# Loading a weight in half rows, and the new plan that goes with it, in an attention and gated-MLP kernel

## The chip, the cores and the metric

The kernel runs on one core of a Trainium2 chip. The metric is the device time of one execution in microseconds, the median of several runs. The engines are PE (matrix multiply), ACT, DVE and POOL (elementwise work) and SP, which here only issues DMAs. The chip has two PE clock levels, 1.2 and 2.4 GHz; the profile gives the granted clock as a share of the higher one.

## The reference

Attention over a band, then a gated MLP on its output, for 8 batches of 576 rows, 8 heads of 64, float32 throughout except `w_in` and `w_out`, which arrive as float64:

```python
scores = scale * np.matmul(q, k.transpose(0, 1, 3, 2))
scores = np.where(masks[None], scores, -1e9)       # band of 32; heads 4 to 7: every 4th of 128
attn = softmax(scores)                             # with 1e-9 added to the sum
x = np.matmul(attn, v)                             # (8, 576, 512) after the heads are joined
h = np.maximum(x @ w_in, 0.0)                      # w_in 512 x 1024
u, v = h[..., :512], h[..., 512:]
v_n = (v - mean(v)) / np.sqrt(var(v) + 1e-6)
v_s = np.einsum('ts,bsd->btd', w_spatial, v_n) + b_spatial[None, :, None]
out = (u * v_s) @ w_out                            # w_out 512 x 512
```

## The kernel before

Everything is kept as a high and a low float32r part, and a product is three matmuls (high-high, high-low, low-high). For each batch the program makes scores and softmax in units of three blocks of 64 rows (`unit`: scores L600, mask L631, the maximum's correction L665, the exponential L675, the transposes L615), weights the values (`weighted`, L750), splits the result into `xth`/`xtl` (`evacuated`, L791 on ACT and the subtraction on DVE), multiplies with the v half of `w_in` (`v_tile`, L815), normalises, multiplies with the u half (`gate`, L882) and with the spatial weights (L892), and projects (`project`, L917). Two head pairs make a group G; a batch has two groups of three units each.

The weights need work of their own before they can be used. A chunk c of `w_in` is 128 rows of 1024 float64 words (1 MB), in two transfers of 64 rows, one to partitions 0 to 63 and one to 64 to 127. `weight` turns one half of a chunk (512 columns, u or v) into float32r parts, in eight steps on ACT (L449, L479, L484), DVE (L453, L455) and, by the table `BY_POOL`, POOL or DVE: an 'a' there puts the addition on POOL (L462) and else on DVE (L465), an 's' puts the subtraction that gives the low part on POOL (L382) and else on DVE (L379). A chunk's staging buffer is given back when both its halves have been read, and then takes the spatial weights and `w_out`.

The order of the instructions on each engine is not the scheduler's. A planner (`Timeline`) holds a cost for each step, picks the next step by its earliest start plus a weight on its rank, and the program keeps the order that comes out; `SHIFTS` adds a number to the rank of each strand, `LOADS` lists the first transfers in the order in which SP is to issue them. Each engine then runs its list in order, and an instruction that waits holds up all behind it. While nothing else is ready in the first 20 us of the plan, `warm` fills PE with products of zeros (L939).

The built program gives the DMAs of SP eight semaphores by turns, and each issue waits until the transfer eight places ahead of it has landed. So no more than eight transfers are under way, whatever their size.

The first loads are, for batch 0: queries and keys (`heads_in`, tile `kq`, 128 partitions), values (`values_in`, tiles `wideh` and `widel`, four transfers of 32 rows of 4,608 bytes for each head pair), and the four chunks of `w_in` (tiles `stage`, `wosl`, `wosh`).

Of the kernel before, what the change touches and what calls it, by code (L numbers as in the profile page):

```python
# [60 lines left out]
LOADS = [0, 1, 17, 4, 2, 21, 18, 14, 3, 16, 8, 15, 5, 13, 20, 6, 9, 19, 22, 7, 11, 12, 10]  # L61
BY_POOL = {
    (0, 0): 'as', (0, 1): 'as', (0, 2): 'a', (0, 3): 'as', (1, 0): 'a', (1, 1): 'as',
    (1, 2): 'as', (1, 3): 'as', (2, 0): 'as', (2, 1): 's', (2, 2): 'as', (2, 3): 'as',
# [165 lines left out]
def tile_banded_attention_gated_moe(  # L230
# [22 lines left out]
    nc = tc.nc  # L253
# [127 lines left out]
    def gsub(out, a, b):  # L381
        nc.gpsimd.tensor_sub(out, a, b.bitcast(F32))  # L382

    staged = {}

    def pieces_in(c):

        yield DMA, 3.0, 1.2  # L390
        tile = stage[c]
        dtype = w_in.dtype
        words = 1 if dtype == F32 else 2
        place = tile[:, : 2 * NF * words]
# [5 lines left out]
        for half in range(2):  # L400
            staged["wi", half, c] = place[:, half * NF * words : half * NF * words + NF * words]
# [647 lines left out]
```

## Time and profile before

| what | value |
|---|---|
| median of 3 runs | 571.76 us (571.36 to 575.04) |
| the profiled execution, its own time | 570.54 us |
| its span, first to last instruction | 568.8 us |
| PE busy | 547.9 us (96%) |
| DVE, ACT, POOL busy | 290.5, 222.5, 140.6 us |
| mean granted PE clock | 0.981 |
| HBM read | 37.79 MB |

The span is what the trace covers; 1.74 us of the execution's time lie around it. PE is the engine that bounds the whole, but a mean over the span hides that its idle time lies at the start, where it waits for data and for the other engines. Waits of the other engines cost nothing unless PE ends up behind them.

### The profile page before, as it was taken

How to read it: one execution, taken by the hardware profiler on the slowest of the kernel's cores; microseconds unless marked ns; L12 is line 12 of the kernel's file. 1: busy time of each engine (PE TensorE's matmuls, PEld its weight loads, DVE VectorE, ACT ScalarE, POOL GpSimd, SP SyncE). 2: the span in 40 equal slices, each digit the busy share in tenths (PEclk: the TensorE clock that was granted, in tenths of full speed). 3: DMA queues.
4: the chain of work that ended last, by engine and by line, in shares of the span. 5: the costliest groups of instructions: out<-in, count | busy, mean ns of one | idle time of the engine just before them, and what ended most of it. 6: DMA issues, size and time to landing. Idle time of an engine off the chain costs nothing.

```text
span 568.8 us, 18036 instructions
## 1 busy us (share of the span) xinstructions
PE 547.9 (96%) x7855; PEld 501.2 (88%) x7855; DVE 290.5 (51%) x728; ACT 222.5 (39%) x558; POOL 140.6 (25%) x168
## 2 busy tenths in 40 slices
PE   8769999999999999999999899999999999999997
PEld 6657889989998878999989898899999988999997
DVE  4758996465344577637444656565414237314220
ACT  2547775344223444325322444334214324224222
POOL 2648782322003442303202314230100013000000
PEclk9759999999999999999999999999999999999999
DMA  8999542330044451021431432410210210000102
GB/s 233 230 274 233 168 119 88 118 86 12 1 129 148 149 139 39 2 81 39 110 94 28 143 99 69 111 50 1 65 42 23 57 40 1 12 21 12 43 22 73
DMA packets 58146, 48.38 MB, mean 85 GB/s; under 512 B 38994, under 2 KB 48210, under 8 KB 57556
## 3 DMA queue, kind: packets, MB, share of 16 engines
q1 hardware_dynamic: 58068, 47.24, 29.4%
q8 instruction: 61, 1.00, 0.7%
q14 instruction: 17, 0.14, 0.1%
HBM read 37.79 MB, written 9.44 MB: 83 GB/s over the span
## 4 chain that ended last, share of the span: by engine, by line
PE 85%; DVE 4%; DMA 4%; issue 3%; ACT 1%; SPq 1%; POOL 1%; POOLq 0%; ACTq 0%; DVEq 0%
PE bank L917 18%; PE bank L815 17%; PE bank L892 16%; PE bank L882 16%; PE bank L750 6%; PE bank L600 5%; PE bank L615 3%; DMA kq<-in_qT_dram 2%; DMA stage<-in_w_in_dram 1%; PE bank L894 1%; PE bank L893 1%; DVE mid L455 1%; PE bank L665 1%; DVE mid L453 1%; DMA stage<-in_w_spT_dram 1%
## 5 line engine op out<-in xcount | busy, mean ns | idle before, releaser
L917 PE MATMUL bank<-gh,woh 128*128 128x288 f32 x256 | 77.8, 304 | 1.1 <-issue 1.1
L882 PE MATMUL bank<-xth,wih 128*128 128x288 f32 x256 | 77.1, 301 | 0.0
L892 PE MATMUL bank<-wth,vnh 128*128 128x288 f32 x256 | 77.0, 301 | 0.0
L917 PE MATMUL bank<-gl,woh 128*128 128x288 f32 x256 | 75.5, 295 | 0.8 <-issue 0.8
L892 PE MATMUL bank<-wtl,vnh 128*128 128x288 f32 x256 | 75.6, 295 | 0.0
L892 PE MATMUL bank<-wth,vnl 128*128 128x288 f32 x256 | 75.5, 295 | 0.0
L882 PE MATMUL bank<-xth,wil 128*128 128x288 f32 x256 | 75.4, 294 | 0.0
L882 PE MATMUL bank<-xtl,wih 128*128 128x288 f32 x256 | 75.4, 294 | 0.0
L917 PE MATMUL bank<-gh,wol 128*128 128x288 f32 x256 | 75.4, 294 | 0.0
L897 DVE TENSOR_TENSOR ur<-ur,bank 128x288 f32<-128x288 f32 x64 | 28.8, 450 | 90.4 <-PE bank L894 90.1
L833 POOL TENSOR_TENSOR stats<-stats,halfneg 128x1 f32<-128x1 f32 (+1 forms) x37 | 25.0, 675 | 156.7 <-DVE stats L831 156.3
L685 POOL TENSOR_TENSOR pg<-pg,nm 128x384 f32<-128x384 f32 x36 | 31.8, 883 | 119.9 <-DVE nm L683 108.4
L815 PE MATMUL bank<-wih,xth 128*128 128x512 f32 (+1 forms) x148 | 61.2, 413 | 0.0
L694 POOL TENSOR_TENSOR pg<-pg,rv 128x384 f32<-128x384 f32 x48 | 41.8, 872 | 77.4 <-DVE rv L692 75.3
L815 PE MATMUL bank<-wil,xth 128*128 128x512 f32 (+1 forms) x148 | 58.1, 393 | 0.0
L815 PE MATMUL bank<-wih,xtl 128*128 128x512 f32 (+1 forms) x148 | 58.0, 392 | 0.0
L921 ACT COPY ob<-bank 128x288 f32<-128x288 f32 x64 | 25.4, 399 | 77.2 <-PE bank L917 59.3
L903 ACT CAST gh<-ur 128x288 fp32r<-128x288 f32 x64 | 27.2, 433 | 61.9 <-DVE ur L897 58.9
L379 DVE TENSOR_TENSOR gl<-ur,gh 128x288 fp32r<-128x288 f32 x64 | 30.3, 481 | 40.9 <-ACT gh L903 40.8
L917 PEld LDWEIGHTS bank<-gh,woh 128*128 128x128 f32 x256 | 48.1, 188 | 2.8 <-issue 1.4
L917 PEld LDWEIGHTS bank<-gl,woh 128*128 128x128 f32 x256 | 48.1, 188 | 1.2 <-issue 1.0
L885 ACT ACTIVATE ur<-bank 128x288 f32<-128x288 f32 x64 | 26.3, 411 | 58.0 <-PE bank L882 57.4
(114 smaller groups left out, 1154.6 us busy)
## 6 DMA issues: line engine op xcount, KB each, us to landing
kq<-in_kT_dram SPq DMA_DIRECT2D x30, 304.0 KB, 3.5
kq<-in_qT_dram SPq DMA_DIRECT2D x30, 288.0 KB, 4.4
val<-in_vw_dram SPq DMA_DIRECT2D x112, 72.0 KB, 2.7
out_dram<-ob SPq DMA_DIRECT2D x48, 144.0 KB, 1.8
stage<-in_w_in_dram SPq DMA_DIRECT2D x4, 512.0 KB, 9.9
stage<-in_w_out_dram SPq DMA_DIRECT2D x4, 512.0 KB, 4.6
out_dram<-ob SPq DMA_DIRECT2D x16, 112.0 KB, 1.8
stage<-in_w_spT_dram SPq DMA_DIRECT2D x5, 288.0 KB, 4.5
```

The source lines that it names most:

```text
L379: nc.vector.tensor_sub(out, a, b.bitcast(F32))
L600: nc.tensor.matmul(s[j][q * QB : q * QB + QB], kq[r, WIN + S :].rearrange("p (u n i t) -> p u t n i", n=2, i=QB, t=US)[:, u, g // 2 % US, ...
L685: nc.gpsimd.tensor_add(flat, flat, nm.unsqueeze(2).broadcast_to([P, 2 * US, KW]))
L694: nc.gpsimd.tensor_mul(flat, flat, rv.unsqueeze(2).broadcast_to([P, 2 * US, KW]))
L750: nc.tensor.matmul(acc[h, j][1][1][i * D : i * D + D, at : at + len(blocks) * QB], values[b, hp][j][r, kb // 2], x, start=phase == 0 and k ...
L815: nc.tensor.matmul(pm, xt[a][:, c, at : at + m], wi[w][:, c, NF:], start=c == 0 and n == 0, stop=c == NC - 1 and n == 2)
L882: nc.tensor.matmul(pu, wi[w][:, c, fs], xt[a][:, c, xs], start=n == 0, stop=n == 3 * NC - 1)
L885: nc.scalar.activation(ur, pu, AF.Relu)
L892: nc.tensor.matmul(pv, vn[c][a][:, fs], wts[w][:, c, ws], start=n == 0, stop=False)
L897: nc.vector.tensor_mul(ur, ur, pv)
L903: nc.scalar.copy(gated[0][:, f, ts], ur)
L917: nc.tensor.matmul(po, wo[w][:, f, ds], gated[a][:, f, ts], start=n == 0, stop=n == 3 * NC - 1)
```

## The change

`w_in` is loaded in half rows: one transfer holds 64 rows of 512 words (256 KB) of one half, and a half chunk of v or u is two transfers. `piece_in(1, c)` loads v's half of chunk c into its own part of a `stage` buffer, which is given back as soon as that half has been read; `piece_in(0, c)` loads u's half into the buffers that `w_out`'s parts take later. The first 64 rows of v's chunk 0 go in four transfers of 8 rows and one of 32. The four transfers of a head pair's values go to partitions 0, 32, 64, 96 in that order, where they went to 0, 64, 32, 96. The costs in the planner, `LOADS`, `BY_POOL` and `SHIFTS` are new, so the order on all engines is.

```diff
 SHIFTS = {
-    0: 0.03, 1: 1.58, 3: -2.17, 5: -4.25, 6: -0.16, 7: -0.65, 8: 0.63, 32: 0.05, 33: 1.3, 34: 1.46,
...
+    0: 1.23, 1: 2.86, 2: 0.22, 3: 0.67, 4: 0.11, 5: 0.41, 6: 0.15, 7: -0.21, 8: -0.19, 36: 1.9,
...
-LOADS = [0, 1, 17, 4, 2, 21, 18, 14, 3, 16, 8, 15, 5, 13, 20, 6, 9, 19, 22, 7, 11, 12, 10]
+LOADS = [0, 1, 3, 20, 2, 10, 21, 4, 5, 15, 8, 6, 13, 9, 12, 18, 7, 22, 23, 11, 19, 17, 26, 24, 16, 14, 25]
 BY_POOL = {
-    (0, 0): 'as', (0, 1): 'as', (0, 2): 'a', (0, 3): 'as', (1, 0): 'a', (1, 1): 'as',
-    (1, 2): 'as', (1, 3): 'as', (2, 0): 'as', (2, 1): 's', (2, 2): 'as', (2, 3): 'as',
+    (0, 0): 's', (0, 1): 'as', (0, 2): 's', (0, 3): 's', (1, 0): 'as', (1, 1): 's',
+    (1, 2): 'as', (1, 3): 'a', (2, 0): 'a', (2, 1): 'a', (2, 2): 'as', (2, 3): 'as',
 }
...
-    def pieces_in(c):
-
-        yield DMA, 3.0, 1.2
-        tile = stage[c]
+    def piece_in(half, c):
+
+        yield DMA, 1.5, 1.1 if half == 0 or c else 2.1
         dtype = w_in.dtype
-        words = 1 if dtype == F32 else 2
-        place = tile[:, : 2 * NF * words]
+        words = NF if dtype == F32 else 2 * NF
+        tile = stage[c // 2 + 2 * (1 - half)]
+        place = tile[:, c % 2 * BIG :][:, :words] if half else tile[:, c % 2 * words :][:, :words]
         for n in range(2):
             row = (c // 2 * 4 + c % 2 + 2 * n) * D
-            nc.sync.dma_start(
-                place[n * D : n * D + D].bitcast(dtype), w_in[row : row + D].rearrange("r h k -> r (h k)")
-            )
-        for half in range(2):
-            staged["wi", half, c] = place[:, half * NF * words : half * NF * words + NF * words]
-        tl.done("in", c)
+            cuts = (0, 8, 16, 24, 32, D) if half and c == 0 and n == 0 else (0, D)
+            for lo, hi in zip(cuts, cuts[1:]):
+                nc.sync.dma_start(
+                    place[n * D + lo : n * D + hi].bitcast(dtype), w_in[row + lo : row + hi, half]
+                )
+        staged["wi", half, c] = place
+        if half:
+            slots["wi", half, c] = [("stage", tile[:, c % 2 * BIG : c % 2 * BIG + BIG])]
+        tl.done("in", "wi", half, c)
...
-        got = yield DMA, 0.64 * (hi - lo), 0.87
+        got = yield DMA, 0.52 * (hi - lo), 0.87
...
-            yield DMA, 1.45, 0.6
+            yield DMA, 1.6, 1.6
             dst = wide[hp // 2][:, hp % 2 * BIG : hp % 2 * BIG + BIG]
-            for n in range(2):
-                k = WIN + (1 - n) * QB
-                for j in range(2):
+            for j in range(2):
+                for n in range(2):
+                    k = WIN + (1 - n) * QB
                     nc.sync.dma_start(dst[j * D + n * QB : j * D + n * QB + QB], vw[b, hp, k : k + QB])
```

The lines of the changed program stand one lower than those of before (L449 is L448 there).

**SP.** Its queue after the last query of the first four head pairs (a transfer of 64x1024 words is half a chunk, one of 64x512 half of a half chunk). Before:

```order
L562 DMA kq_78<-in_qT_dram 128x576
L397 DMA wosl<-in_w_in_dram 64x1024 x2
L576 DMA wideh<-in_vw_dram 32x1152 x4
L397 DMA stage_65<-in_w_in_dram 64x1024 x2
L576 DMA wideh<-in_vw_dram 32x1152 x4
L576 DMA widel<-in_vw_dram 32x1152 x4
L397 DMA wosh<-in_w_in_dram 64x1024 x2
L576 DMA widel<-in_vw_dram 32x1152 x4
```

After:

```order
L561 DMA kq_78<-in_qT_dram 128x576
L398 DMA wosh<-in_w_in_dram 64x512 x2
L575 DMA wideh<-in_vw_dram 32x1152 x4
L398 DMA stage_64<-in_w_in_dram 8x512 x4
L398 DMA stage_64<-in_w_in_dram 32x512
L398 DMA stage_64<-in_w_in_dram 64x512
L398 DMA stage_65<-in_w_in_dram 64x512 x2
L398 DMA stage_64<-in_w_in_dram 64x512 x2
L575 DMA widel<-in_vw_dram 32x1152 x4
L575 DMA wideh<-in_vw_dram 32x1152 x4
L575 DMA widel<-in_vw_dram 32x1152 x4
```

All of v's half now stands ahead of the last three head pairs' values, and three of u's four half chunks behind them; the piece that is split (`stage_64`, v's chunk 0) is the third of `w_in`, behind v's chunk 2 (which stands at the place of the first chunk of before), u's chunk 1 and one head pair's values.

**ACT.** The exponentials (`pg`) and the first step of a weight (`mid<-` a staging tile) from the first group's last unit on. Before:

```order
L449 ACTIVATE mid_86<-wosl 128x512
L707 COPY pT_88<-bank_70 128x384
L675 ACTIVATE pg<-bank_68 128x3x64
L675 ACTIVATE pg<-bank_69 128x3x64
L479 ACTIVATE wosl<-wosl 128x512
L484 CAST wih<-mid_87 128x512
L707 COPY pT_88<-bank_72 128x384
L449 ACTIVATE mid_82<-wosl 128x512
```

After:

```order
L448 ACTIVATE mid_86<-stage_64 128x512
L483 CAST wih<-mid_85 128x512
L674 ACTIVATE pg<-bank_68 128x3x64
L674 ACTIVATE pg<-bank_69 128x3x64
L706 COPY pT_88<-bank_72 128x384
L674 ACTIVATE pg<-bank_71 128x3x64
L674 ACTIVATE pg<-bank_74 128x3x64
L478 ACTIVATE stage_64<-stage_64 128x512
```

In both, a read of a freshly loaded weight stands ahead of the second group's first exponential; what it waits for is now the split piece.

**DVE.** Around the subtractions that follow the first group's values (`xtl`). Before:

```order
L379 TENSOR_TENSOR xtl<-bank_67,xth 128x288
L453 TENSOR_SCALAR mid_87<-mid_86 128x512
L455 SCALAR_TENSOR_TENSOR mid_87<-mid_86,mid_87 128x512
L453 TENSOR_SCALAR mid_83<-mid_82 128x512
L379 TENSOR_TENSOR xtl<-bank_69,xth 128x288
```

After:

```order
L378 TENSOR_TENSOR xtl<-bank_74,xth 128x288
L454 SCALAR_TENSOR_TENSOR mid_85<-mid_84,mid_85 128x512
L452 TENSOR_SCALAR mid_83<-mid_82 128x512
L464 ISA mid_84<-stage_64,mid_85 128x1024
L454 SCALAR_TENSOR_TENSOR mid_83<-mid_82,mid_83 128x512
L464 ISA mid_82<-wosl,mid_83 128x1024
L378 TENSOR_TENSOR xtl<-bank_68,xth 128x288
```

The additions of two weights (L464) now stand on DVE between the two groups' subtractions, where POOL did them.

## Rows read from the trace of the kernel before

**Rows 1.** Windows by stage: PE, PEld, DVE, ACT, POOL busy, granted clock, DMA share, GB/s

```profile
0.00:15.00 15.00, 12.28 (x182) 9.33 (x182) 7.37 (x29) 4.84 (x9) 3.56 (x15) 1.00 0.88 241
15.00:30.00 15.00, 10.53 (x181) 8.57 (x179) 9.83 (x23) 6.60 (x15) 8.82 (x8) 0.73 1.01 226
30.00:41.30 11.30, 7.94 (x169) 7.07 (x170) 7.33 (x16) 4.57 (x13) 5.46 (x5) 0.50 1.00 258
41.30:60.00 18.70, 18.70 (x360) 13.86 (x359) 14.69 (x27) 13.87 (x30) 13.97 (x13) 0.97 0.87 225
60.00:90.00 30.00, 28.20 (x459) 25.43 (x460) 28.99 (x59) 21.44 (x53) 22.68 (x22) 1.00 0.53 165
90.00:568.80 478.80, 470.28 (x6513) 436.91 (x6511) 222.27 (x576) 171.15 (x443) 86.11 (x106) 1.00 0.21 61
```

**Rows 2.** Waits of PE from 0 to 41.3 us: total, times, longest

```profile
PE bank L750 <- issue: 3.1, 1, 3.1
PE bank L600 <- issue: 2.7, 1, 2.7
```

**Rows 3.** Timeline of PE, 26 to 45 us: start, length, instruction

```profile
32.79 1.50 PE L750 MATMUL bank<-pT,wideh 32*64 32x64 f32 x72
...
38.53 1.00 PE L750 MATMUL bank<-pT,wideh 32*64 32x64 f32 x46 [3.10 <-issue]
39.47 2.18 PE L615 MATMUL bank<-ident,pg 128*128 128x128 f32 x9
41.30 0.78 PE L815 MATMUL bank<-wih,xth 128*128 128x512 f32 x1
```

**Rows 4.** Windows of 3 us, columns as in rows 1

```profile
11.00:14.00 3.00, 1.32 (x51) 0.90 (x51) 1.65 (x4) 2.41 (x6) 0.42 (x1) 1.00 1.05 401
...
23.00:26.00 3.00, 3.00 (x64) 2.49 (x63) 2.90 (x8) 1.89 (x6) 0.95 (x2) 1.00 1.02 222
28.00:31.00 3.00, 1.46 (x16) 1.29 (x16) 0.91 (x3) 0.00 (x0) 1.34 (x2) 0.62 1.00 253
...
40.00:43.00 3.00, 3.00 (x13) 2.71 (x12) 1.66 (x5) 2.83 (x8) 0.00 (x0) 0.61 1.04 393
```

**Rows 5.** Waits of SP, 0 to 60 us

```profile
SPq L576 <- DMA stage<-in_w_in_dram: 3.9, 2, 2.0
```

**Rows 6.** Timeline of ACT, 0 to 62 us

```profile
11.59 0.66 ACT L449 ACTIVATE mid<-stage 128x512 f32<-128x512 f32 x1 [9.36 <-DMA stage<-in_w_in_dram]
...
22.41 0.66 ACT L449 ACTIVATE mid<-wosl 128x512 f32<-128x512 f32 x1 [0.35 <-DMA wosl<-in_w_in_dram]
23.96 0.48 ACT L707 COPY pT<-bank 128x384 f32<-128x384 f32 x1 [0.89 <-PE bank L615]
24.36 0.64 ACT L675 ACTIVATE pg<-bank 128x192 f32<-128x192 f32 x2
```

**Rows 7.** Timeline of DVE, 0 to 90 us

```profile
12.29 0.43 DVE L453 TENSOR_SCALAR mid<-mid 128x512 uint32<-128x512 uint32 x1 [4.88 <-ACT mid L449]
...
22.71 0.62 DVE L660 TENSOR_REDUCE nm<-bank 128x3 f32<-128x192 f32 x2 [2.28 <-PE bank L600]
23.25 0.55 DVE L690 TENSOR_REDUCE sm<-pg 128x6 f32<-128x384 f32 x1
```

**Rows 8.** The values' tile, 0 to 40 us: issues on SP, first and last start

```profile
L576 SPq DMA_DIRECT2D wideh<-in_vw_dram x8: 311/317/582, 13.0 to 23.5; - x8
...
DMA to landing us min/median/max: 8.0/9.8/10.1
```

**Rows 9.** Groups by form, 0 to 90 us: busy, mean ns, idle before

```profile
L455 DVE SCALAR_TENSOR_TENSOR mid<-mid,mid 128x512 uint32<-128x512 uint32 x12 | 11.3, 945 | 0.3
...
L453 DVE TENSOR_SCALAR mid<-mid 128x512 uint32<-128x512 uint32 x12 | 9.7, 811 | 8.1 <-ACT mid L449 8.1
...
L462 POOL TENSOR_TENSOR mid<-mid,stage 128x512 uint32<-128x512 uint32 x7 | 9.1, 1302 | 14.7 <-DVE mid L455 13.3 <-ACT stage L479 0.7 <-ACT mid L449 0.7
```

**Rows 10.** The addition that DVE makes before, L465

```profile
L465 DVE CUSTOM_DVE_ANT_0 mid<-stage,mid x1: 694/694/694, 76.5 to 76.5; 128x1024 uint16<-128x1024 uint16 x1
```

More of the change, by code (lines that the diff above doesn't have):

```diff
@@ L416, in read @@
     def read(key):
-        if key[0] == "wo":
-            tl.give(*slots[key])
-        else:
-            c = key[2]
-            tl.tally(("read", c), 2, [("chunk", c)], [("stage", stage[c][:, n * BIG : n * BIG + BIG]) for n in range(2)] if c < 2 else [])
+        tl.give(*slots.get(key, ()))
+        tl.done("read", *key)
     def weight(key, dtype, pool):
-        yield [("in", *key), ("chunk", 2), ("chunk", 3)] if key[0] == "wo" else [("in", key[2])]
+        yield [("in", *key)] + [("read", "wi", 0, c) for c in range(NC)] * (key[0] == "wo")
         yield "mid" if dtype == F32 else "wk mid mid"
@@ L949, in tile_banded_attention_gated_moe @@
     first = [heads_in(0, hp, lo, hi) for lo, hi in ((0, 1), (1, NU)) for hp in (0, 1)]
-    first += [pieces_in(0), heads_in(0, 2), values_in(0, 0), values_in(0, 1), heads_in(0, 3), pieces_in(1)]
-    first += [values_in(0, 2), values_in(0, 3), pieces_in(2), pieces_in(3)]
+    first += [heads_in(0, 2), heads_in(0, 3), piece_in(1, 0), values_in(0, 0), values_in(0, 1), piece_in(1, 1)]
+    first += [piece_in(1, 2), values_in(0, 2), values_in(0, 3), piece_in(1, 3)] + [piece_in(0, c) for c in range(NC)]
     first += [spatial_in(c) for c in range(5)] + [weight_in(c) for c in range(NC)]
```

57 rows, old and new, of the table SHIFTS are left out of this document.

## The prediction

> **What bounds the kernel now.** I read the windows by stage first. From 41.3 us on PE is busy for 18.70 of 18.7, 28.20 of 30 and 470.28 of 478.8 us: it bounds the run, and the order there can only move crumbs about. Before 41.3 us it is idle for 2.7 + 4.5 + 3.4 = 10.6 us, and a part of what counts as busy is the filler of zeros or work at a granted clock of 0.73 and 0.50 (15 to 30 and 30 to 41.3 us) [rows 1]. PE's work after that point is the same in both programs, so what the change is worth is read here: how much earlier than 41.30 us can the first product with `w_in` (L815) start [rows 3], and does what comes behind it keep pace. Next, what PE waited for: 3.1 and 2.7 us for its own instructions [rows 2], and otherwise its chain is late because the others are. So I followed ACT, which sat 9.36 us until the first chunk of `w_in` had landed at 11.5 us [rows 6], and DVE, which waited 4.88 us behind ACT with the maxima of two units queued behind its instruction [rows 7]. Both are waits for data, so the last view is the DMA's.
>
> There the reader should see two rates. While queries and keys (128 partitions) move, it is 401 and 393 GB/s; in the stretch of `w_in` (64 partitions each) 222, and in that of the values (32 each) 253, with the engines' share at 1.0 in all of them [rows 4]. The engines are never idle there, they are slower. Since the share is 1.0 in the stages from 15 to 41.3 us too [rows 1], arrival is bytes over rate there.
>
> **Bytes ahead of what is needed.** The first product needs the values of head pairs 0 and 1, v's half weights and all softmax units of group 0. In the changed queue the later of these two (`wideh`, the last line but one of SP's new rows) has ahead of it and with it 2,368 KB of queries and keys, five half chunks of 512 KB and three head pairs' values of 576 KB: 6,656 KB. In the old one it was 2,368, three whole chunks of 1,024 and two head pairs of 576: 6,592 KB, which had landed at 23.5 + 8.0 = 31.5 us [rows 8]. So for the values, half rows save nothing by themselves: at the old rate they land at about 31.5 + 64 KB/0.23 = 31.8 us. What comes earlier at any rate is v's half as a whole (in after 5,504 KB, where the last chunk was in after 8,192), and the first piece: 512 KB where 1,024 stood, so ACT's first read starts an estimated (11.5 - 4)/2 = 3.7 us earlier, and the maxima of units 1 and 2 behind it on DVE with it. That gain is passed on only to the next wait, which is again for a weight: ACT's read of the split piece stands ahead of all exponentials of group 1. Up to that piece the new queue holds 4,480 KB; in the old one 4,416 KB had landed when ACT read `wosl` at 22.41 us, after 0.35 us of waiting [rows 6]. So this read is at about 22.6 us in both programs, whatever the skew does later.
>
> From there the new ACT order has 0.66 (read) + 0.66 (cast, taken as long as the read) + 0.64 + 0.48 + 0.64 us [rows 6], both exponentials done at 25.7; then 0.55 and 0.62 us of DVE work and more like it [rows 7] and PE's last correction, about 28 us before the weighting (L750) can start. It started at 32.79 us before [rows 3].
>
> **Out of step.** Between the split piece and those values lie two half chunks and two head pairs, 2,176 KB or 2.23 MB. If all transfers from there on move at 393 GB/s, they take 5.7 us, and the values are there at 22.6 + 5.7 = 28.3 us; at 230 (between 222 and 253) 9.7 us, 32.3. The trace shows no transfer of 64 partitions at the higher rate, so this is bounded from both sides by those rows. I take the higher one: the values, whose four transfers alternated between low and high partitions, went at 253 and not 222, so overlap of the halves helps a little already, and eight rows can occupy at most eight of the sixteen engines if a row stays whole, so four such transfers leave those eight behind the others by as much as an engine moves of one 64-row transfer (four rows). Then the weighting starts at 28.3 us, limited by values and softmax alike, 4.5 us earlier.
>
> That the 8-row transfers load only half of the engines is what the Trainium skill states (DMA: Bandwidth & Descriptors, "Why a DMA increments its semaphore by 16 and not by 1": the largest number up to 16 that divides the outer sizes); no row here shows it.
>
> **Behind the weighting.** Before, nine transposes (2.18 us at half clock) stood between it and L815 [rows 3]; in the new order three of them stand between its phases or earlier, so 0.7 us less. The wait for instructions of 3.10 us inside the weighting [rows 3] I leave as it is; it may go from 0 to 3.1.
>
> **BY_POOL.** Three additions and one subtraction move from POOL to DVE, 4 x 0.69 = 2.8 us [rows 10], and DVE is the fullest engine behind PE where they land: 28.99 of 30 us between 60 and 90 [rows 1]. Against that, POOL loses 4 x 1.30 us [rows 9], beside which DVE's own instructions are slow: L453 takes 811 ns in the mean where it takes 0.43 alone [rows 7], L455 945 where 0.69 would do (as L465, the same size); 12 x 0.38 + 12 x 0.26 = 7.7 us over 21 POOL instructions of weights, 0.37 each, so 1.5 us come back. Net +1.3 us, on the path because DVE has no room there; bounds -1.5 and +2.8.
>
> The rest costs nothing: SP issues 12 more transfers, but each waits for a landing anyway (L576 waited 3.9 us for two of them [rows 5]), so issue time is covered as long as eight transfers in flight hold enough bytes. The filler shrinks from 35 to 18 products in the built order, in time in which PE has nothing else; if that lets the clock fall earlier, the units between 9 and 15 us run at half speed, an estimated 1 us. The late part of the plan is as full as before, within 1 us either way.
>
> **Sum.** -4.5 - 0.7 + 1.3 = -3.9 us against the profiled execution's 570.54, 566.6. That execution lies 1.22 below the median, so the forecast is 567.8 us.
>
> **The rivals.**
> *The halves stay in step.* Then the values come at 32.3 us, 0.5 earlier than the weighting started, and the sum is -0.5 - 0.7 + 1.3: 571.9 us, no change. For it: between 15 and 41.3 us transfers to low and high partitions were under way together, eight at a time, and the rate was 226 and 258 GB/s [rows 1]. Against it: none of those was made uneven. This is the Trainium skill's rule (SBUF — State Buffer, "Can I just issue two DMAs to hit both halves?"): two concurrent DMAs to the two halves serialize, with 6% gained. By that rule the trace agrees so far (222 against 401).
>
> *More than the sum.* If the queue drains faster, PE's wait of 3.1 us for instructions inside the weighting goes too [rows 3], and with PE filled from 33 us the clock is back 2 us earlier (it was 0.50 up to 41.3 [rows 1]): another 5.1 us, 562.7. For it: those fetches use the same DMA engines. Against it: the wait of 2.7 us [rows 2] came in a burst of the smallest matmuls, which is there in both.
>
> *Slower.* Eight transfers in flight may now hold too little: four of them are 32 KB and twelve in a row 144 KB. While the 8-row pieces go, they occupy part of the engines and the others run dry behind the eighth place; the split half chunk then takes twice its 2.3 us, ACT's read of it and all of group 1 are 2.3 us later, and with the halves in step and DVE's full 2.8 us the sum is -0.5 - 0.7 + 2.3 + 2.8 = +3.9: 575.7 us. It decides if the split piece lands later than about 24.5 us.
>
> **How the numbers follow.** Forecast (567.8) 0.42; in step (571.9) 0.27; more (562.7) 0.17; slower (575.7) 0.14. Each is uncertain by some 2 us. The range that leaves out no more than 2 in 10 goes from 562.5 to 574.5: all of the first two, half of the others. About 1% is what a measurement of this kernel tells from no change (the three runs before spread over 0.6%), so faster is below 566.0 and slower above 577.5: faster 0.17 + 0.12 of the forecast's 0.42 = 0.29, slower 0.04, the same 0.67.
>
> **What would show it.** In the new profile: 1 us of transfers to half the partitions at over 330 GB/s after the split piece (forecast) or under 260 (in step); ACT's read of `stage_64` at 22 to 23 us; the first weighting at 28 to 29 us and the first product with `w_in` at 36 to 37; DVE over 90% busy in the 30 us behind it. I am wrong if the units of group 1 no longer wait for that piece, if PE idles again after 41 us because DVE falls behind, or if the late part of the plan differs by more than 1 us.

## The result, and the profile after

The changed kernel takes 566.01 us (median; 565.31 to 567.0), the kernel before beside it 571.91 (571.36 to 575.04): a ratio of 0.9887, with a 95% interval of 0.9848 to 0.9926, so 5.9 us or 1.1% less. The profiled execution takes 566.32 us, its span is 564.5; before they were 570.54 and 568.8. The two profiles hold 4.2 of the 5.9 us, since that of before lies 1.37 us under its median and that of the changed kernel 0.31 above. The sum of the prediction was 566.6 for the profiled execution, and its forecast for the median 567.8.

The windows by stage of the kernel after, columns as in [rows 1], which answer to them (the last one ends with the shorter span):

```profile
0.00:15.00 15.00, 11.58 (x220) 8.57 (x220) 9.78 (x37) 5.41 (x12) 5.80 (x17) 1.00 0.86 245
15.00:30.00 15.00, 8.58 (x137) 6.34 (x134) 9.37 (x24) 7.52 (x17) 7.25 (x7) 0.82 0.84 210
30.00:41.30 11.30, 8.50 (x236) 6.57 (x236) 4.05 (x10) 4.93 (x12) 3.64 (x3) 0.63 1.02 244
41.30:60.00 18.70, 16.15 (x231) 13.02 (x232) 14.58 (x26) 12.29 (x26) 12.23 (x12) 0.91 0.90 253
60.00:90.00 30.00, 25.90 (x351) 22.78 (x350) 29.18 (x56) 19.06 (x43) 19.19 (x20) 1.00 0.40 126
90.00:564.50 474.50, 470.03 (x6670) 439.40 (x6668) 224.16 (x584) 173.28 (x452) 86.25 (x106) 1.00 0.22 64
```

The reader should see three things. The rates up to 60 us are about the old ones, 210 to 253 GB/s (225 to 258 before). PE idles more than before between 41.3 and 90 us: 2.55 us where it was nothing, then 4.10 where it was 1.80. And behind 90 us it idles less: 474.50 - 470.03 = 4.47 us, where it was 8.52 [rows 1].

Windows of 3 us around and behind the split piece in the kernel after:

```profile
23.00:26.00 3.00, 1.49 (x51) 0.93 (x41) 2.27 (x6) 3.00 (x9) 2.11 (x2) 1.00 0.96 240
26.00:29.00 3.00, 1.40 (x7) 0.93 (x7) 2.95 (x7) 1.96 (x5) 1.50 (x2) 0.85 1.02 230
28.00:31.00 3.00, 0.00 (x0) 0.00 (x0) 2.70 (x6) 0.62 (x1) 2.27 (x2) 0.52 1.02 235
32.00:35.00 3.00, 2.45 (x71) 2.16 (x71) 0.00 (x0) 0.49 (x2) 0.69 (x1) 0.50 0.96 234
```

That is the rate of transfers in step: 222 and 253 GB/s before, against 393 and 401 for queries and keys [rows 4]. No window shows anything out of step.

The timeline of PE in the kernel after, which answers to [rows 3] (L749 and L814 were L750 and L815):

```profile
31.10 0.48 PE L749 MATMUL bank<-pT,wideh 32*64 32x64 f32 x4 [3.69 <-DMA wideh<-in_vw_dram]
32.42 2.05 PE L749 MATMUL bank<-pT,wideh 32*64 32x64 f32 x68 [0.84 <-DMA wideh<-in_vw_dram]
...
37.23 0.79 PE L814 MATMUL bank<-wih,xth 128*128 128x512 f32 x1
...
41.63 0.35 PE L749 MATMUL bank<-pT,widel 32*64 32x64 f32 x11 [1.06 <-ACT turnstile L762]
43.71 0.92 PE L749 MATMUL bank<-pT,widel 32*64 32x64 f32 x69 [1.73 <-issue]
```

and that of ACT, to [rows 6]:

```profile
8.49 0.66 ACT L448 ACTIVATE mid<-stage 128x512 f32<-128x512 f32 x1 [6.27 <-DMA stage<-in_w_in_dram]
...
22.13 0.67 ACT L448 ACTIVATE mid<-stage 128x512 f32<-128x512 f32 x1 [2.33 <-DMA stage<-in_w_in_dram]
```

The first product with `w_in` starts at 37.23 us, 4.07 earlier than before. The way there is another than forecast: the weighting starts 1.69 us earlier (the values came at 31.1 and 32.4 us, and PE sat waiting for them), and from there to the first product it takes 6.13 us instead of 8.51, since the wait of 3.10 us for instructions [rows 3] isn't there; one of 1.73 stands further on.

The waits of PE from 60 us to the end, total, times, longest; in the kernel before:

```profile
PE bank L750 <- issue: 2.0, 2, 1.3
PE bank L917 <- issue: 1.9, 2, 1.1
PE bank L615 <- POOL pg L694: 0.8, 2, 0.5
...
PE bank L600 <- issue: 0.6, 1, 0.6
...
```

and after:

```profile
PE bank L614 <- POOL pg L693: 3.2, 3, 1.9
PE bank L630 <- DVE vnl L378: 0.8, 2, 0.4
...
```

Before, PE waited there 2.0 + 1.9 + 0.6 = 4.5 us for its own instructions; after, not at all, but 3.2 us for the softmax's `pg` from POOL.

So the time can be read as two numbers of each execution: when the first product with `w_in` starts, and how long what follows takes. Before: 41.30 + 527.5 = 568.8 us; after: 37.23 + 527.3 = 564.5. Nearly the whole difference, 4.07 of 4.3 us, stands in the first number. The second is the same only in sum: more waiting up to 90 us, less behind it. PE's clock is in it as well: from the first product to 60 us the granted clock was 0.97 before and 0.90 after.

What I held after these readings: the split and the turns do nothing; the lead at the start is lost again up to 90 us on DVE and POOL, which work on the weights there (DVE is busy for 29.18 and POOL for 19.19 of the 30 us from 60 on); and the gain of the run is made behind 90 us, where the new order has no wait for instructions. The rivals: the split is the gain (the prediction's step), or what comes earlier at the start stays to the end, whoever is full, and the order behind matters by itself. The numbers of the theories below are those of each experiment.

### The profile page after: what moved, and what is told of

Same layout as the page of the kernel before. It is cut to its first block, busy times and chain, and to the rows that moved or that the text cites. A ratio compares the mean times of both kernels' runs of the same rounds, so it can differ in the third digit from the quotient of the medians.

```text
span 564.5 us, 18030 instructions
## 1 busy us (share of the span) xinstructions
PE 540.7 (96%) x7838; PEld 496.7 (88%) x7838; DVE 291.1 (52%) x732; ACT 222.5 (39%) x558; POOL 134.4 (24%) x164
## 4 chain that ended last, share of the span: by engine, by line
PE 81%; DMA 10%; DVE 4%; SPq 3%; issue 1%; POOL 1%; ACT 0%; ACTq 0%
PE bank L916 18%; PE bank L891 17%; PE bank L881 17%; PE bank L814 15%; PE bank L749 5%; PE bank L599 4%; DMA kq<-in_qT_dram 3%; DMA wideh<-in_vw_dram 3%; PE bank L614 2%; PE bank L893 1%; PE bank L892 1%; DMA stage<-in_w_spT_dram 1%; DMA wosl<-in_w_in_dram 1%; DMA stage<-in_w_in_dram 1%; SPq L398 1%
## 5 line engine op out<-in xcount | busy, mean ns | idle before, releaser
L832 POOL TENSOR_TENSOR stats<-stats,halfneg 128x1 f32<-128x1 f32 (+1 forms) x37 | 26.2, 709 | 156.8 <-DVE stats L830 156.3
L814 PE MATMUL bank<-wih,xth 128*128 128x512 f32 (+1 forms) x148 | 61.2, 414 | 0.0
L814 PE MATMUL bank<-wih,xtl 128*128 128x512 f32 (+1 forms) x148 | 58.6, 396 | 0.0
L814 PE MATMUL bank<-wil,xth 128*128 128x512 f32 (+1 forms) x148 | 58.5, 396 | 0.0
L891 PEld LDWEIGHTS bank<-wth,vnh 128*128 128x128 f32 x256 | 48.1, 188 | 1.0 <-ACT ur L884 0.3
L881 PEld LDWEIGHTS bank<-xth,wih 128*128 128x128 f32 x256 | 48.1, 188 | 0.7
```

The lines of the kernel that those rows point to most:

```text
L814: nc.tensor.matmul(pm, xt[a][:, c, at : at + m], wi[w][:, c, NF:], start=c == 0 and n == 0, stop=c == NC - 1 and n == 2)
L832: nc.gpsimd.tensor_tensor(rs[:m], rs[:m], halfneg[:m], op=ALU.pow)
L881: nc.tensor.matmul(pu, wi[w][:, c, fs], xt[a][:, c, xs], start=n == 0, stop=n == 3 * NC - 1)
L891: nc.tensor.matmul(pv, vn[c][a][:, fs], wts[w][:, c, ws], start=n == 0, stop=False)
```

## The experiments

Unless said otherwise each is the changed program with one edit that leaves the order on PE, ACT, DVE and POOL as it is. Ratios are to the kernel before, with their 95% intervals; the changed kernel's is 0.9887.

**The split piece in one.**

```diff
-            cuts = (0, 8, 16, 24, 32, D) if half and c == 0 and n == 0 else (0, D)
+            cuts = (0, D)
```

> The changed program with its first half chunk in one piece: v's chunk 0 goes in two transfers of 64 rows, and no transfer of 8 or 32 rows is made. The order on PE, DVE, ACT and POOL is that of the changed program. Theory 1 (the split takes nothing out of step, since transfers moved at 230 to 240 GB/s behind it as before): the time stays at the changed program's 566.0 us, within 0.7 us, the rate from 23 to 35 us stays at 230 to 240 GB/s, and ACT reads the piece at 22 us, if anything up to 0.3 us sooner. Theory 2 (the split is what the gain of 5.9 us comes from, as the prediction had it): the rate falls below 225 GB/s, the first weighting comes later than 33 us, and the time goes back to 570 us or more.

565.4 us, ratio 0.9897 (0.9864 to 0.9929). The four windows of 3 us from 23 us on show 232, 205, 203 and 241 GB/s, ACT read the piece at 22.56 us, and the first weighting starts at 30.14 us. The split is worth nothing in the time: theory 1. One sign of theory 2 did show, a rate under 225 GB/s (from 26 to 31 us, with an engines' share of 0.86 and 0.77 and not 1.02); why is open, and the values came no later for it.

**The old turns of the values.**

```diff
-            for j in range(2):
-                for n in range(2):
-                    k = WIN + (1 - n) * QB
+            for n in range(2):
+                k = WIN + (1 - n) * QB
+                for j in range(2):
```

> The changed program with the four transfers of a head pair's values in their old order (to partitions 0, 64, 32, 96). Theory 1 (the turns take nothing out of step): no difference, 566.0 us within 1, 230 to 240 GB/s from 23 to 35 us, the first weighting at 31 us within 0.5. Theory 2 (turns matter): the values land a microsecond or more later and the time is 567 us or more.

565.68 us, 0.9895 (0.9859 to 0.9931); 256, 251, 242 and 238 GB/s in the four windows, first weighting at 29.57 us. Theory 1 in the time; the values came rather earlier, within what arrival varies by from execution to execution (29.07 to 31.10 us in four that differ ahead of it in nothing but the split, the turns and some products of zeros).

**u's halves behind v's, chunk by chunk.**

```diff
-        for n in range(2):
+        for n in range(2 * half):
...
+            nc.sync.dma_start(stage[c // 2 + 2][n * D : n * D + D, c % 2 * words :][:, :words].bitcast(dtype), w_in[row : row + D, 0])
```

> The changed program with the u half of each chunk of w_in issued row block by row block right behind v's half, so that whole chunks arrive in turn as before the change; the order on PE, DVE, ACT and POOL stays that of the changed program. The values of head pair 0 then have 8,192 KB ahead of and with them instead of 6,656: at 235 GB/s 6.7 us later, so the first weighting comes at 37 to 38 us (it is at 31.1 in the changed program) and the first product with w_in at 42 to 44 (37.2). Theory 1 (the lead of the start is lost by 90 us because DVE, ACT and POOL are full with the weights there, and the gain comes later): part of the 6.7 us is taken up before 90 us, and the time is 567 to 570 us. Theory 2 (what comes earlier at the start stays as gained to the end, so v's half ahead of u's is the gain): all of it stays, 572 to 573 us, slower than the kernel before.

573.93 us, 1.0040 (1.0018 to 1.0062): 7.9 us slower than the changed kernel and slower than the kernel before. The delay is larger than I worked out, and at another place. ACT's timeline:

```profile
33.67 0.66 ACT L448 ACTIVATE mid<-wosh 128x512 f32<-128x512 f32 x1 [16.45 <-DMA wosh<-in_w_in_dram]
```

The changed order reads u's chunk 1 early (at 15.97 us), and here it comes with the last chunk; DVE's steps on that weight and the maxima of group 1 stand behind that read (PE waited 13.51 us for them). First weighting 40.97, first product 45.46 us, 8.2 later than in the changed kernel; the span is 6.6 longer. So of the 8.2 us by which the first product starts later, 6.6 are left in the span and 7.9 in the median, which is theory 2, and the new order needs the new loads.

**`w_in` in transfers of 128 rows.** The rows are laid out so that a half chunk is one transfer.

```diff
...
-            for lo, hi in zip(cuts, cuts[1:]):
-                nc.sync.dma_start(
-                    place[n * D + lo : n * D + hi].bitcast(dtype), w_in[row + lo : row + hi, half]
-                )
+        nc.sync.dma_start(place.bitcast(dtype), w_in[c * P : c * P + P, half])
...
```

> The changed program with the rows of w_in laid out so that each half chunk is one transfer of 128 rows to 128 partitions; the order on PE, DVE, ACT and POOL is that of the changed program, and the values still go in transfers of 32 rows. This shows what the forecast hoped for from the split: w_in at the rate of queries and keys. Five half chunks ahead of the values of head pair 0 at 393 instead of 235 GB/s save 4.5 us, so the first weighting comes at 26.5 to 28 us, ACT's read of v's chunk 0 at 19 to 20. Theory 1 (a lead at the start is lost by 90 us on DVE and POOL): the first product with w_in comes 2 to 4 us earlier than 37.2 us, but the time is 564.5 to 566.5 us. Theory 2 (a lead stays): 561 to 563 us.

561.27 us, 0.9815 (0.9788 to 0.9843). First weighting at 26.16 us, first product at 31.85, 5.4 earlier, and the span is 5.6 shorter: theory 2 again. This is the size of the step that the prediction had hung on the split. PE's waits between 28 and 90 us in it, total, times, longest:

```profile
PE bank L599 <- DMA kq<-in_qT_dram: 4.8, 2, 4.5
PE bank L614 <- POOL pg L693: 1.6, 1, 1.6
PE bank L749 <- issue: 0.6, 1, 0.6
```

**The values too.** Each head pair's values of batch 0 in one transfer of 128 rows, without the half that nothing reads, on top of the last edit (lines from there on are two lower: L747, L812).

```diff
...
-                    nc.sync.dma_start(dst[j * D + n * QB : j * D + n * QB + QB], vw[b, hp, k : k + QB])
-            values[b, hp] = [dst.rearrange("p (t j d) -> p t j d", j=2, d=D)[:, :, j] for j in range(2)]
+            nc.sync.dma_start(dst, v0[hp])
+            values[b, hp] = [dst.rearrange("p (t d) -> p t d", d=D)] * 2
...
```

> The program with w_in in full-width transfers (128 rows, the third experiment, 561.3 us), and the values of batch 0 as well: each head pair's in one transfer of 128 rows of 2,304 bytes, without the half of each row that nothing reads. The order on PE, DVE, ACT and POOL stays. Values of head pair 0 then have 1,770 KB less time at 240 GB/s and 885 KB at 393 instead ahead of them, 5 us sooner. Theory 1 (with w_in at full rate the values are no longer what comes last; ACT's steps and the softmax are): the 1.3 us that PE still waited for wideh go, and the time is 560 to 561.5 us. Theory 2 (arrival still sets the start): first weighting 4 to 5 us earlier and 556 to 558 us.

557.13 us, 0.9748 (0.9705 to 0.9790), the fastest version, 8.9 us under the changed kernel. Theory 1 fell: with these loads in earlier, the first weighting starts at 22.59 us, 3.6 earlier (theory 2 had 4 to 5), and shows no wait for the values. Half the bytes and wider transfers go together here; what each gives isn't shown. Windows and PE's timeline of it:

```profile
15.00:18.00 3.00, 2.94 (x68) 2.47 (x69) 2.39 (x7) 2.68 (x6) 1.12 (x2) 1.00 1.02 409
...
23.00:26.00 3.00, 1.89 (x101) 1.44 (x89) 2.93 (x7) 2.26 (x6) 2.03 (x2) 1.00 1.04 398
```

```profile
22.59 1.05 PE L747 MATMUL bank<-pT,wideh 32*64 32x64 f32 x72
...
27.36 0.74 PE L747 MATMUL bank<-pT,wideh 32*64 32x64 f32 x34 [2.40 <-issue]
28.61 0.79 PE L812 MATMUL bank<-wih,xth 128*128 128x512 f32 x1
```

I had left out that pieces of `w_in` stand behind values in the queue. They come earlier as well, and with them what ACT does behind them: the first exponentials of group 1 at 17.88 us, where they were at 20.82 with `w_in` alone in 128 rows.

**Batch 1's keys ahead in SP's queue**, on top of `w_in` in 128 rows: spatial weights and an early load of batch 6 are held back until batch 1's first two head pairs are issued.

```diff
+    def send(to, src, b=6): held.append((to, src)) if b > 5 and (1, 1) not in keys else nc.sync.dma_start(to, src)
...
-        nc.sync.dma_start(kq[:, kc], kT[b, hp, :, kc])
+        send(kq[:, kc], kT[b, hp, :, kc], b)
...
+        while (b, hp) == (1, 1) and held:
+            nc.sync.dma_start(*held.pop(0))
```

> The program with w_in in full-width transfers (561.3 us), with SP's queue changed at one place: batch 1's first queries and keys stand ahead of the spatial weights and of a head pair of batch 6 that is loaded early. The order on the other engines stays. PE waited 4.46 us for these keys at 50.2 us. Theory 1 (behind 45 us PE is the bound, and a wait taken away there is kept to the end): 556.5 to 558 us. Theory 2 (POOL and DVE, full with the weights between 60 and 90 us, take the place of that wait): PE waits longer for pg, 3 us or more between 45 and 90 us, and the time is 560 to 561.5 us.

565.75 us, 0.9881 (0.9838 to 0.9925): 4.5 us slower than without (3.8 by the ratios), and outside the ranges of both theories. Its waits of PE between 28 and 90 us, to be held against those of the program with `w_in` in 128 rows:

```profile
PE bank L749 <- issue: 3.7, 1, 3.7
PE bank L614 <- POOL pg L693: 3.5, 3, 1.9
PE bank L664 <- DVE nm L659: 2.8, 1, 2.8
...
```

The wait for the keys is gone, and in its place are `pg` at the same three places as in the changed kernel (theory 2), 2.8 us for a maximum from DVE (`nm`), and 3.7 us for instructions inside the first weighting, which neither theory had. That one was there with other transfers under way in it; whether the moved keys made it long isn't shown. With the values in 128 rows as well:

> Both of these together: w_in and batch 0's values in full-width transfers, and batch 1's first queries and keys ahead in SP's queue. Theory 1 (a lead is handed on to the end by PE): 555 to 557.5 us. Theory 2 (POOL and DVE give it back before 90 us): 559.5 to 561 us.

557.26 us, 0.9745 (0.9707 to 0.9783): no gain over the values alone, which had no wait for keys at that place left, and pg's waits of 3.0 us from 60 to 90 us in both. Theory 1's numbers are met without its reason.

**128 more instructions on PE.** The page of before lists, under its DMA queues, one for instructions (packets, MB, share of the 16 engines):

```profile
q8 instruction: 61, 1.00, 0.7%
```

These are packets of some 16 KB. PE has 15,710 matmuls and weight loads, 257 to a packet; that the queue is PE's is read from these counts. Such packets are the blocks meant below. The first try put 64 products ahead of the filler:

```diff
+        for _ in range(64): nc.tensor.matmul(got[0][1][:, :4], z, z[:, :4], start=True, stop=True)
```

> The changed program with 64 small products of zeros (4 columns each) put ahead of the filler, where PE waits for the first data; everything else is in its order. They take about 4 us at the very start at most and shift PE's instructions by 128 against the blocks of 16,384 bytes in which they are fetched (256 instructions of 64 bytes). Theory 1 (the changed program gained in the middle because its order, by the place of these blocks, leaves no wait for instructions behind 60 us, where the program before had 4.5 us of them): such waits come back, 2 to 5 us behind 60 us, and the time is 568 to 571 us. Theory 2 (the gain has nothing to do with the blocks): still no waits for instructions behind 60 us, and 566.0 us within 0.8.

572.39 us, 1.0007 (0.9986 to 1.0028). It is no clean test: a product of 4 columns took 0.22 us with its weight load of 128 columns, 13.8 us in all and not 4, and the softmax began that much later (the first product with `w_in` only 1.4 us later). Waits for instructions of 2.3 and 1.3 us came up behind 45 us. The second try puts small ones (32 x 4) ahead of the first weighting, in the changed program and in the one before:

```diff
...
+                for _ in range(64 * (b == G == 0)): nc.tensor.matmul(acc[0, 0][1][1][:32, :4], few, few[:, :4], start=True, stop=True, skip_group_check=True)
```

> The changed program with the same 64 small products of zeros ahead of its first weighting, where PE waits for the values (27 to 31 us). Theory 1 (the changed order has no wait for instructions behind 60 us only as long as the blocks' edges fall where they do): 2 to 5 us of such waits come up behind 45 us, and the time is 568 to 571 us. Theory 2 (the places of the edges don't matter): none come, and the time is 566.0 us within 0.8. A wait for instructions that PE has at 43.7 us (1.73 us) may go by theory 1, which would give that much back.

570.54 us, 0.9983 (0.9958 to 1.0008), 4.5 us slower than the changed kernel, although the first product starts at 35.15 us, 2.1 earlier. PE's waits from 41.3 us on:

```profile
PE bank L749 <- issue: 5.1, 3, 3.8
PE bank L614 <- POOL pg L693: 3.5, 3, 1.9
...
```

5.1 us for instructions, where the changed program has the one of 1.73. Theory 1. Not all of the 4.5 us need be these waits: the profiled execution lies 2.0 us under the median, and its granted clock from the first product to 60 us is 0.82 where the changed program has 0.90.

> The kernel before with 64 small products of zeros (32 x 4 columns, a weight load and a product each, so 128 instructions) put ahead of the first weighting, where PE waits for the values (27 to 32.8 us). Its instructions behind them stand half a fetched block (16,384 bytes, 256 instructions of 64 bytes) further on; the products are estimated at 2 to 4 us, inside that wait. Theory 1 (PE's waits for its own instructions behind 60 us, 4.5 us in six places, come from where the blocks' edges fall): they go from those places; what comes in other places is between 0 and 4.5 us, and the time goes with it, 567 to 572 us. Theory 2 (they belong to the work that stands there): the six waits stay at the same products, 4 to 5 us in all, and the time is that of the kernel before within 1 us.

569.56 us, 0.9955 (0.9937 to 0.9974): a shift of 128 instructions alone makes the old program some 2 us faster (1.6 by the medians, 2.6 by the ratio). The wait of 3.10 us inside the first weighting [rows 3] is gone, and the first product came at 38.88 us, 2.4 earlier, though of that lead only 0.2 is left in the span of the profiled execution; the waits behind 60 us (five in the view above, where I had counted six) went or moved, and from 41.3 us on there are 4.9 us in five places at L750 and 1.0 at L882. Theory 1: the waits move when the instructions are shifted, so they belong to the place and not to the work; from 41.3 us on they did not get shorter in all (5.9 us against 4.5).

**The weights' steps on their old engines.**

```diff
-            nc.vector.tensor_add(f, g, low)
+            (nc.gpsimd if "a" in was_by else nc.vector).tensor_add(f, g, low)
...
-            gsub(lo, w, hi)
+            (gsub if "s" in was_by else sub)(lo, w, hi)
```

> The changed program with the additions and subtractions of the weights on the engines on which they stood before (net three additions and one subtraction go back from DVE to POOL), each at its place in the program's order; PE's and ACT's orders stay the same. The prediction put the move to DVE at a cost of 1.3 us (bounds: a gain of 1.5 and a cost of 2.8). Theory 1 (DVE is the engine that holds PE between 41 and 90 us): the time falls by about 1.3 us, to 564 to 565. Theory 2 (POOL holds it: PE waited 4.7 us for pg from POOL before 90 us): more of these waits, PE waits for pg 6 us or more before 90 us, and the time is 567 to 570 us.

568.45 us, 0.9938 (0.9913 to 0.9963), 2.4 us slower than the changed kernel (the intervals just overlap; the old turns, on the same chip, gave 565.68). So the move from POOL to DVE gained, as theory 2 has it. That it gained by shorter waits for `pg` is not shown. PE's waits over the whole run begin with:

```profile
PE bank L614 <- POOL pg L693: 7.3, 3, 3.5
...
```

It was 4.7 us over the whole run after. But the longest of them stands ahead of the first weighting, for which PE then waits for the values as in the changed program:

```profile
25.72 0.55 PE L614 MATMUL bank<-ident,pg 128*128 128x128 f32 x3 [3.47 <-POOL pg L693]
...
30.92 0.48 PE L749 MATMUL bank<-pT,wideh 32*64 32x64 f32 x4 [3.80 <-DMA wideh<-in_vw_dram]
```

The first product starts at 37.12 us, no later than in the changed program (37.23). Behind it the waits for `pg` come to 3.8 us against 3.2, and before 90 us to 5.2, less than the 6 that theory 2 asked for. The profiled execution lies 2.6 us over the median, and what it has more behind the first product is hardly idle time of PE (12.0 us against 11.9) but busy time (520.0 against 515.4), with a granted clock of 0.72 and not 0.90 from the first product to 60 us. Why the clock was lower isn't shown.

**The old numbers.** The planner's `SHIFTS` of before, each at its own strand, with the new loads; the order on all engines is a third one.

```diff
-    0: 1.23, 1: 2.86, 2: 0.22, 3: 0.67, 4: 0.11, 5: 0.41, 6: 0.15, 7: -0.21, 8: -0.19, 36: 1.9,
...
+SHIFTS = {0: 0.03, 1: 1.58, 3: -2.17, 5: -4.25, 6: -0.16, 7: -0.65, 8: 0.63, 36: 0.05, 37: 1.3, 38: 1.46,
...
```

> The changed program with the planner's table of numbers (SHIFTS) of before, each put to the strand to which it belonged; the loads in half rows, LOADS, BY_POOL and the costs are the changed ones. So the planner makes a third order, for the new loads, with numbers that weren't chosen for it. Theory 1 (part of the gain is in the numbers, that is in an order whose blocks of instructions and whose POOL work fall well): waits for instructions and for pg come to 5 us or more behind 45 us, and the time is 568 to 574 us. Theory 2 (the loads alone make the gain, whatever the order): 565 to 567 us.

602.54 us, 1.0527 (1.0488 to 1.0567). Theory 1 in kind and far beyond its size. The first product with `w_in` starts at 35.64 us, earlier than in the changed kernel, and what follows takes 565.1 us and not 527.3: PE idles 34.6 us in it, where it idled 11.9, and is busy for 15 us more, at a mean granted clock of 0.957 over the span (0.984 in the changed kernel). The largest of PE's waits from 41.3 us on (L569 is the scores, L584 the transposes there):

```profile
PE bank L569 <- DMA kq<-in_qT_dram: 9.4, 4, 4.3
PE bank L584 <- POOL pg L663: 5.9, 2, 4.4
PE bank L784 <- DVE xtl L348: 3.1, 1, 3.1
PE bank L569 <- issue: 3.0, 3, 1.8
...
```

All profiled executions by the two numbers:

| program | first product, us | from there to the end, us |
|---|---|---|
| before | 41.30 | 527.5 |
| before, 128 instructions more | 38.88 | 529.7 |
| after | 37.23 | 527.3 |
| piece in one | 35.72 | 527.5 |
| old turns | 35.31 | 529.1 |
| u behind v | 45.46 | 525.6 |
| `w_in` in 128 rows | 31.85 | 527.1 |
| values too | 28.61 | 526.6 |
| keys ahead | 35.05 | 529.1 |
| values and keys | 29.27 | 527.9 |
| 64 products first | 38.61 | 533.0 |
| after, 128 instructions more | 35.15 | 531.7 |
| old engines | 37.12 | 532.1 |
| old numbers | 35.64 | 565.1 |

What is loaded how moves the first number over 16.9 us and the second over 3.5 (525.6 to 529.1). Against the changed kernel, leads of 5.4, 8.0 and 8.6 us at the first product are 5.6, 7.3 and 9.3 in the span; but leads of 1.5 (piece in one), 1.9 (old turns) and 2.2 (keys ahead) are 1.3, 0.1 and 0.4, so a lead of that size isn't safe. The instructions' places move both numbers, the old numbers above all the second.

Two cautions: each row is one execution, up to 2.6 us from its program's median, and PE's clock is in the second number. In the three rows with 533.0, 532.1 and 531.7 the granted clock from the first product to 60 us is 0.68, 0.72 and 0.82, where the changed kernel has 0.90. So that POOL's share or the instructions' places alone make these rows longer isn't shown.

## Why the prediction came out right, point by point

**What bounds the kernel.** Right: a lead at the first product with `w_in` is a lead at the end, by 5.4 to 5.6 us with `w_in` in 128 rows and 8.6 to 9.3 with the values too. What I held after reading the trace, that DVE and POOL swallow it, fell for leads of that size; of 1.9 and 2.2 us (old turns, keys ahead) nearly nothing was left.

**Bytes ahead of what is needed.** Right. ACT's first read came 3.1 us earlier (forecast 3.7), the read of the split piece at 22.13 us (about 22.6), and the values at 31.1 to 32.4, which is the sum at the old rate (32.3).

**Out of step.** This is the step that failed: "I take the higher one" (393 GB/s behind the split). The transfers went at 230 to 240, and the program without the split is as fast. The term of -4.5 us for the weighting's start measured -1.7. What the mechanism would have given is real, 4.7 us of the median with `w_in` in 128 rows, but uneven pieces don't buy it. The rival in step had the rate right: 230 to 240 GB/s with halves by turns, 397 to 409 with all 128 partitions in one transfer. The Trainium skill states this rival's rule (SBUF — State Buffer, "Can I just issue two DMAs to hit both halves?"): two concurrent DMAs to the two halves serialize. The trace agrees.

**Behind the weighting.** "The wait for instructions of 3.10 us inside the weighting [rows 3] I leave as it is" was mis-sized: that wait was gone (one of 2.31 us stands ahead of the weighting, at 17.35 us), and with the fewer transposes the way from the weighting to the first product shrank by 2.4 us where -0.7 stood. -1.7 - 2.4 makes the 4.07 us, where -4.5 - 0.7 = -5.2 was forecast: the start came out near it by other causes, which is luck.

**BY_POOL.** +1.3 us had the wrong sign. Undoing it costs 2.4 us, 0.9 beyond the bound of -1.5. The move was costed by DVE's busy time (29.18 of 30 us from 60 to 90, as full as forecast), and that did not hold the run up; by what the relief of POOL gained is open, as the experiment on it shows. Two sizes were off besides. Of DVE's groups up to 90 us after:

```profile
L452 DVE TENSOR_SCALAR mid<-mid 128x512 uint32<-128x512 uint32 x12 | 5.9, 492 | 10.2 <-ACT mid L448 10.2
...
L464 DVE CUSTOM_DVE_ANT_0 mid<-wosl,mid 128x1024 uint16<-128x1024 uint16 x2 | 3.0, 1504 | 2.8 <-ACT wosl L478 2.7
...
L464 DVE CUSTOM_DVE_ANT_0 mid<-wosh,mid 128x1024 uint16<-128x1024 uint16 x1 | 1.3, 1321 | 0.0
L464 DVE CUSTOM_DVE_ANT_0 mid<-stage,mid 128x1024 uint16<-128x1024 uint16 x1 | 0.7, 692 | 0.1
```

Three of the four additions took 1.3 to 1.5 us each and not 0.69, and each of these three overlapped a subtraction on POOL (L381), which the one of 0.69 did not. And L452 (L453 before) took 492 ns in the mean, where it had taken 811; with the old split it took 555, so that most of this fall is not the move's doing.

**The late part.** "As full as before, within 1 us either way" failed twice over: from 41.3 to 90 us PE idles 2.55 + 2.30 = 4.85 us more, behind 90 us 4.05 less. That the two nearly cancel made the sum right, by luck too: in the span -1.7 (start of the weighting) - 2.4 (from there to the first product) - 0.2 (what follows) = -4.3 us stands where -4.5 - 0.7 + 1.3 = -3.9 was forecast, and no term has its forecast size. Two of the prediction's own signs of being wrong came in part true: PE idles again after 41 us, and the late part differs by more than 1 us. That the late part came from the place of the blocks' edges is shown as far as shifts by 128 instructions make such waits go and come in both programs; that those waits were avoided by choice of numbers is not.

**The rivals.** In step: its rate and its landing times held, its time (571.9) didn't, since the wait of 3.10 us for instructions went and the move off POOL gained where it was summed as a loss. More than the sum: its wait of 3.1 us did go, though the queue drained no faster. Slower: the split piece was in time, so its point of 24.5 us wasn't reached.

What stays open is why POOL's `pg` is late at the same three places, most often between 60 and 90 us, in most of these programs, what sets PE's clock behind the first product (0.68 to 0.97 up to 60 us), and how much of the 2.55 us from 41.3 to 60 us is the new order's doing: 1.73 of it is one wait for instructions, which other executions have elsewhere.

## What to carry to other kernels

Read such a time as two numbers, the start of the first work that fills the bounding engine and the length of what follows, and cost a change to each apart: with the order kept, loads moved the first over 16.9 us and the second over 3.5, while a new order or shifted instructions moved both. To use both halves of the partitions, make one transfer span them; pieces of uneven size by turns don't. And an engine's busy time alone doesn't say whether it can take more: work moved from POOL to a DVE that was busy for 29.18 of 30 us gained 2.4 us. With an order that is planned in detail, 128 idle instructions cost 4.5 us and another table of rank numbers 36.5, against the 5.9 that the whole change gains. A sum that comes out right isn't proof of its terms: read each one in the new trace.

## What the runs showed of the hardware that was not expected

Behind four 8-row pieces the rate was 230 to 240 GB/s, and 203 to 241 without them: nothing near the 393 of queries and keys either way, and no loss by small pieces. Transfers of 128 rows in place of those of 64 and 32 took the rate from 210 to 365 GB/s over 15 to 30 us when values and `w_in` both had it; with the values still in 32 rows behind `w_in` in 128, the rate fell to 166 GB/s at an engines' share of 0.62 (26 to 29 us); that eight such transfers in flight were too little fits this, but was not tested. PE's waits for its own instructions are up to 3.9 us each (in the shifted program of before), and 128 instructions more ahead of them move them to other places.
